# Single accumulation banks handed out by the ordering pass, per-head maxima, last 768 tokens by 384, new bookings

## The chip, the cores and the metric

The kernel runs on one core of a Trainium2 chip. The metric is the device time of one execution in microseconds (us). TensorE (PE in the profile) does the matrix products and the transposes, VectorE (DVE) and ScalarE (ACT) the elementwise work and all copies out of PSUM, SyncE (SP) issues the DMAs. GpSimd builds some constants at the start and does nothing else.

## The reference

Attention with a memory term, then two feed-forward layers, all float32:

```python
# per batch (4) and head (8): S = 576 tokens, D = 64
scores = q @ k.T / 8, causal mask, minus the row's maximum
a      = exp(scores); a /= a.sum(-1) + 1e-9
local  = a @ v
q_p    = where(q > 0, q, exp(q) - 1) + 1
mem    = (q_p @ M_prev) / (q_p . z_prev + 1e-6)
x      = sigmoid(beta) * mem + (1 - sigmoid(beta)) * local   # 2304 tokens x 512
h = x @ w_in;  x = (h * tanh(softplus(h))) @ w_out            # 512 -> 2048 -> 512
h = x @ w_in2; out = (h * cos(h)) @ w_out2                    # 512 -> 2048 -> 512
```

## The kernel before

Two heads make a pair; 16 pairs (four of each batch) are worked one after the other. For each pair q and k are loaded and transposed on TensorE (tiles ptq, ptk), scores of five row blocks are made in three slots (tile s, `f_sc`; the mask is added by small products, line 495), VectorE takes the row maxima (tile nm, `f_mx`), ScalarE the exponentials with their sums (tile p, `f_ex`), VectorE scales the rows (line 572) and writes the memory columns (line 549). The blocks of p are then transposed (tile t, `flip`, 30 transposes for a pair), copied out into PT by ScalarE or VectorE, and multiplied with v and M_prev (tile pv). The result xs goes to DRAM (x1d).

The first layer runs in two parts. `block0` ("phase 0") takes blocks of 256 tokens through the first 8 of the 16 slices of 128 hidden units: products into h (line 759), copy to g, the activation, a split of g into a high and a low half G, products into acc (line 802), and the partial sums to DRAM (xad). `late` with p = 1 ("phase 1") takes blocks of 384 tokens through the other 8 slices (lines 887 and 967) and adds the partial sum (line 978); with p = 2 ("phase 2") it does the second layer, all 16 slices (lines 887 and 969). Each float32 product is three passes of split operands. Weights are loaded and decoded by five operations each (`weight`, lines 125 to 142); those of slices 8 to 15 can only be placed once the attention's memory is given back (`f_host`).

No engine's order is written by hand. Every operation is a task with engine(s), a booked cost, dependences, a rank and the buffers that it takes; `arrange` lets a greedy pass run over a booked clock and emits, on each engine, the ready task of lowest rank. Attention ranks before phase 0, phase 0 before phases 1 and 2, so phase 0 fills what the pass books as idle on TensorE. Tasks marked "act/dve" go to whichever engine is free in the books. A class of buffers has a fixed number of places (`slots_of`); in PSUM the eight banks are split by class: sc 2 places of two banks, misc 2, h 1, acc 1. Until the first phase-0 product, `arrange` puts dummy products (line 303, tile warm) where the booked load of TensorE is low. Once emitted, each engine takes its instructions strictly in that order.

## Time and profile before

| | |
|---|---|
| three timed runs | 1083.94, 1082.56, 1082.08 us; median 1082.56 us |
| profiled execution, first to last instruction (span) | 1080.1 us; it comes with no other time of its own, and the timed runs lie 2.0 to 3.8 us above its span |
| TensorE busy | 1053.2 us (98%), 6938 products |
| VectorE busy | 761.6 us (71%) |
| ScalarE busy | 570.1 us (53%) |
| attention (last pv ends) | 373 us |
| phase 0 ends, phase 1 begins | 481 us |
| phase 2's first acc product | 686 us |

Engines work at the same time, so their busy times do not add up. Products are pipelined: a row's mean duration is the time from a product's start to its end, and the next one starts before that end; how fast products really follow each other is read from a run of them in the chain of waits (its length divided by its count). A wait names the instruction that waited and the one that released it.

### The profile page before, as it was taken

The numbers are of one execution on the slowest core, as the hardware profiler recorded it, in microseconds if no ns is written. First come the engines' busy times: TensorE is split into PE (matmuls) and PEld (weight loads), VectorE is DVE, ScalarE is ACT, GpSimd is POOL, SyncE is SP. The second block draws the span as 40 slices with busy tenths as digits, with TensorE's granted clock in tenths as the row PEclk, the third lists the DMA queues.
The fourth block names the chain that finished last, engine by engine and source line by source line (L and its number), as shares of the span: only waits on it lengthen the run. The fifth ranks groups of instructions, "written<-read, shape, count | busy, mean of one in ns | idle before, by whom it ended". The sixth has DMA issues, their size and how long they took to land.

```text
span 1080.1 us, 17930 instructions
## 1 busy us (share of the span) xinstructions
PE 1053.2 (98%) x6938; PEld 938.7 (87%) x6938; DVE 761.6 (71%) x1694; ACT 570.1 (53%) x1279; POOL 3.8 (0%) x19
## 2 busy tenths in 40 slices
PE   8898999999999999999999999999999999999998
PEld 5666778788877899989999999998999999999997
DVE  6999997886787568757552228887666676766664
ACT  4676675676676443433323234766555555555544
POOL 1000000000000000000000000000000000000000
PEclk9999999999999999999999999999999999999999
DMA  6455423222322165446352216211000010000000
GB/s 165 114 132 161 113 55 103 69 70 67 100 69 59 44 204 156 137 135 205 102 183 88 89 59 187 79 38 59 1 30 30 1 59 2 30 30 1 30 1 30
DMA packets 112853, 88.73 MB, mean 82 GB/s; under 512 B 65792, under 2 KB 103680, under 8 KB 112768
## 3 DMA queue, kind: packets, MB, share of 16 engines
q1 hardware_dynamic: 112768, 87.58, 27.1%
q8 instruction: 55, 0.90, 0.3%
q14 instruction: 30, 0.25, 0.1%
HBM read 68.69 MB, written 18.87 MB: 81 GB/s over the span
## 4 chain that ended last, share of the span: by engine, by line
PE 88%; DVE 7%; ACT 3%; issue 1%; POOL 0%; ACTq 0%; POOLq 0%; DVEq 0%
PE h L887 28%; PE acc L969 18%; PE acc L967 9%; PE h L759 9%; PE acc L802 9%; PE pv L654 5%; PE t L587 4%; PE s L491 3%; DVE nm L520 2%; DVE p L572 1%; PE warm L303 1%; ACT p L536 1%; PE ptq L400 1%; ACT PT L315 1%; PE ptk L400 1%
## 5 line engine op out<-in xcount | busy, mean ns | idle before, releaser
L887 PE MATMUL h<-x,w 128*128 128x384 f32 x1728 | 345.0, 337 | 1.6 <-ACT g L903 1.6
L887 PEld LDWEIGHTS h<-x,w 128*128 128x128 f32 x1728 | 307.4, 188 | 17.2 <-ACT g L903 1.8
L969 PE MATMUL acc<-w,G 128*128 128x512 f32 x864 | 228.4, 393 | 0.0
L969 PEld LDWEIGHTS acc<-w,G 128*128 128x128 f32 x864 | 160.0, 188 | 22.1
L954 DVE TENSOR_TENSOR G<-g,G 128x384 fp32r<-128x384 f32 x144 | 79.8, 555 | 100.2 <-ACT G L315 99.6
L759 PE MATMUL h<-x,w 128*128 128x256 f32 x864 | 127.7, 288 | 4.6 <-DVE g L317 4.2
L802 PE MATMUL acc<-G,w 128*128 128x256 f32 x864 | 129.7, 289 | 1.1 <-ACT o L315 0.7
L759 PEld LDWEIGHTS h<-x,w 128*128 128x128 f32 x864 | 111.4, 191 | 9.0 <-DVE g L317 5.2
L315 ACT ACTIVATE G<-g 128x384 fp32r<-128x384 f32 (+1 forms) x152 | 81.2, 535 | 66.6 <-DVE g L938 35.8
L802 PEld LDWEIGHTS acc<-G,w 128*128 128x128 f32 x864 | 111.9, 191 | 4.0 <-ACT o L315 1.4
L967 PE MATMUL acc<-G,w 128*128 128x384 f32 x576 | 112.6, 336 | 0.0
L536 ACT ACTIVATE p<-s,nm 128x64 f32<-128x64 f32 (+4 forms) x160 | 81.3, 515 | 40.0 <-DVE nm L520 26.2
L967 PEld LDWEIGHTS acc<-G,w 128*128 128x128 f32 x576 | 100.9, 188 | 0.0
L931 ACT ACTIVATE n<-n 128x384 f32<-128x384 f32 x96 | 49.9, 521 | 63.5 <-DVE n L927 63.5
L903 ACT ACTIVATE g<-h 128x384 f32<-128x384 f32 x48 | 23.4, 491 | 113.1 <-PE h L887 112.2
L587 PE MATMUL t<-ident,p 128*128 128x128 f32 (+1 forms) x480 | 73.7, 277 | 7.8 <-ACT PT L315 3.7
L520 DVE TENSOR_REDUCE nm<-s 128x2 f32<-128x1024 f32 (+4 forms) x80 | 62.2, 790 | 23.5 <-PE s L495 16.4
L915 DVE TENSOR_SCALAR u<-hs 128x384 f32<-128x384 f32 x96 | 34.5, 359 | 54.6 <-ACT hs L315 51.9
L938 DVE TENSOR_TENSOR g<-n,hs 128x384 f32<-128x384 f32 x96 | 53.2, 555 | 26.3 <-ACT n L934 26.2
L587 PEld LDWEIGHTS t<-ident,p 128*128 128x128 f32 (+1 forms) x480 | 52.3, 140 | 18.5 <-ACT PT L315 7.8
L315 ACT ACTIVATE hs<-h 128x384 f32<-128x384 f32 x96 | 47.0, 490 | 39.3 <-PE h L887 36.6
L315 ACT ACTIVATE PT<-t 128x256 f32<-128x256 f32 (+3 forms) x97 | 43.4, 466 | 42.0 <-PE t L587 41.5
(91 smaller groups left out, 1243.6 us busy)
## 6 DMA issues: line engine op xcount, KB each, us to landing
raw<-in_moe_w_in_dram SPq DMA_DIRECT2D x32, 512.0 KB, 4.3
raw<-in_moe_w_out_dram SPq DMA_DIRECT2D x32, 512.0 KB, 3.8
k<-in_k_dram SPq DMA_DIRECT2D x32, 144.0 KB, 2.8
x1d<-xs SPq DMA_DIRECT2D x32, 144.0 KB, 2.1
xad<-o SPq DMA_DIRECT2D x9, 512.0 KB, 3.7
x2d<-o SPq DMA_DIRECT2D x6, 768.0 KB, 3.6
x<-x2d SPq DMA_DIRECT2D x6, 768.0 KB, 4.2
out_dram<-o SPq DMA_DIRECT2D x18, 256.0 KB, 2.0
```

What stands on the lines that cost most here:

```text
L315: nc.scalar.activation(dst, src, AF.Copy, scale=1.0 if scale is None else scale)
L520: nc.vector.tensor_reduce(out=s["nm"][:, c], in_=s["sp"][i], axis=AX.X, op=ALU.max, negate=True)
L536: nc.scalar.activation(d["p", i][:, j, D + lo:D + hi], src, AF.Exp, bias=s["nm"][:, c, j:j + 1], scale=1.0, accum_out=s["sm"][:, 1 if part ...
L587: nc.tensor.transpose(ps[:, at:at + r], d["p", i][0:r, h, j * P:(j + 1) * P], ident[0:r, 0:r])
L654: nc.tensor.matmul(o[h * D:(h + 1) * D, z_ - lo:w], vt[:, h, j - 1, :] if j else d["mv"][:, h, :], PT[:, c + z_:c + hi], start=j == 0, sto ...
L759: nc.tensor.matmul(h[:, half // 2], w[:, a, 0, c * P:(c + 1) * P], x[:, e_, c, :], start=c == 0 and pi == 0, stop=c == NKC - 1 and pi == 2)
L802: nc.tensor.matmul(t[:, c], w[:, a, 1, n * P:(n + 1) * P], G[:, e_, half], start=f == 0 and pi == 0 and c == 0, stop=f == NFH - 1 and pi == 2,
L887: nc.tensor.matmul(q_["h"], w[:, a, 0, c * P:(c + 1) * P], x[:, e_, c, :], start=c == 0 and pi == 0, stop=c == NKC - 1 and pi == 2)
L938: nc.vector.tensor_tensor(out=q_["g"], in0=q_["n"], in1=q_["hs"], op=ALU.mult)
L954: ENG[e].tensor_tensor(out=q_["G"][:, 1], in0=q_["g"], in1=q_["G"][:, 0].bitcast(F32), op=ALU.subtract)
L967: nc.tensor.matmul(o, w[:, a, 1, c * P:(c + 1) * P], G[:, e_, :], start=st, stop=sp_)
L969: nc.tensor.matmul(o, G[:, a, c * P:(c + 1) * P], w[:, e_, 1, :], start=st, stop=sp_)
```

## The change

Five things are changed. (1) The fixed split of PSUM goes; `arrange` hands out eight single banks, with a cap for each class (`CAP`). (2) The scores of a pair's two heads stand in two banks taken one by one, the maximum is taken per head (two reductions of half the width in place of one), all maxima of a slot stand in the books ahead of the exponentials, and the exponentials of a head need only that head's maxima. (3) `block0` runs over 6 blocks of 256 tokens (1536 tokens) in place of 9; the last 768 tokens go through all 16 slices in blocks of 384, as the first two blocks of phase 1, without a partial sum. (4) Costs and latencies in the books are others, and instructions of VectorE and ScalarE may overlap by `NEXT`. (5) On TensorE a ready task of the same array mode (scores, pv, all others) now goes first whatever its rank (`KEEP`).

```diff
-    SEM, SWITCH, TABLE, WAIT = 0.1, 0.12, 1.3, 2.5
-    RATE, LAND = 160.0, 2.0
+    CAP = {"warm": 1, "sc": 4, "misc": 3, "h": 2, "acc": 4, "hB": 3}
+    def bank(b, name):
+        return pools["bank"][b.bank].tile([P, 512], F32, tag="b", name=name)
+    SEM, SWITCH, TABLE, WAIT = 0.035, 0.1, 1.28, 2.5
+    RATE, LAND, KEEP = 160.0, 2.0, 10000.0
+    TAIL = {"pe": 0.16, "act": 0.0, "dve": 0.0, "sp": 0.0, "host": -SEM}
+    NEXT = {"pe": 0.0, "act": -0.1, "dve": -0.09, "sp": 0.0, "host": 0.0}
...
+                    for x, o in enumerate(banks):
+                        y = clear(o) if x not in used else None
+                        if y is not None and (f is None or y < f):
+                            f, b.bank = y, x
+                    if n[b.cls] >= CAP[b.cls]:
+                        return None
...
+                    if e == "pe" and t.mode == mode:
+                        rank -= KEEP
...
-            bs, bp, bn = Buf("sc"), Buf("pt"), Buf("nm")
+            bs, bp, bn = [Buf("sc"), Buf("sc")], Buf("pt"), Buf("nm")
...
-                nc.vector.tensor_reduce(out=s["nm"][:, c], in_=s["sp"][i], axis=AX.X, op=ALU.max, negate=True)
+            for j in range(2):
+                for c, i in enumerate(SLOTS[x]):
+                        nc.vector.tensor_reduce(out=s["nm"][:, c, j:j + 1], in_=s["sp", i, j], axis=AX.X, op=ALU.max, negate=True)
+                maxed[j] = t_m
...
-    FS = (range(0, NFH), range(NFH, NF), range(0, NF))
-    blocks = [(p, j) for p in range(3) for j in range(NT // TBS[p])]
-    N0 = NT // T0
+    N0 = 6
+    NS = N0 * T0 // T1
+    JS = [*range(NS, N1), *range(NS)]
+    blocks = [(0, j) for j in range(N0)] + [(p, j) for p in (1, 2) for j in JS]
+    def FS(p, j):
+        return range(NA if p == 0 else NF) if p != 1 or j >= NS else range(NA, NF)
...
-                  "raw": 3, "dec": 2, "x": 2, "o2": 1, "hB": 3, "G2": 3, "g2": 2, "hs": 4, "u": 2, "n": 3,
-                     "acc1": 1, "acc2": 1, "acc3": 1, **{f"w{f}": 1 for f in range(NF)}})
```

How the instructions stand on the engines, before and after, at three places. First VectorE, from the first maximum of pair 12 on (nm12_0 and nm12_1 are the maxima of its first two slots). Before:

```order
L520 TENSOR_REDUCE nm12_0_3814<-s12_0_3789 128x2 x2
L317 COPY xs11_3800<-pv11_1_3803 128x288
L428 TENSOR_SCALAR mn13_3832<-q13_3775 128x640
L317 CAST G0_3_0_3837<-g0_3_0_3551 128x512
L317 CAST G0_3_1_3844<-g0_3_0_3551 128x512
L779 TENSOR_TENSOR G0_3_0_3837<-g0_3_0_3551,G0_3_0_3837 128x512
```

The same place after the change, where s12_0_0 and s12_0_1 are the banks of the two heads:

```order
L553 TENSOR_REDUCE nm12_0_3542<-s12_0_0_3510 128x1 x2
L553 TENSOR_REDUCE nm12_1_3548<-s12_1_0_3528 128x1
L553 TENSOR_REDUCE nm12_0_3542<-s12_0_1_3511 128x1
L355 COPY PT11_3501<-t11_4_3550 128x4x128
L355 COPY PT11_3501<-t11_4_3565 128x256
L553 TENSOR_REDUCE nm12_0_3542<-s12_0_1_3511 128x1
```

Each row block's maximum is two instructions, and the phase-0 work between (G0_3: block 3) is gone from here. Second TensorE, among the transposes of pair 11, before (acc0_2 and h0_3 belong to phase-0 blocks 2 and 3):

```order
L587 MATMUL t11_2_3730<-ident_85,p11_2_3635 128x128 x3
L802 MATMUL acc0_2_1_3607<-G0_2_3_3481,w0_6_1853 128x256 x6
L587 MATMUL t11_2_3746<-ident_85,p11_2_3635 128x128 x3
L587 MATMUL t11_1_3750<-ident_85,p11_2_3635 128x128 x2
L802 MATMUL acc0_2_1_3607<-G0_2_3_3481,w0_7_2005 128x256 x6
L587 MATMUL t11_1_3761<-ident_85,p11_2_3635 128x128 x2
L400 MATMUL ptq12_1_3765<-ident_85,q12_3463 128x128 x2
L759 MATMUL h0_3_1_3571<-x3_2724,w0_3_1262 128x256 x6
```

And after:

```order
L625 MATMUL t11_4_3565<-ident_85,p11_1_3394 128x128 x2
L803 MATMUL h0_2_0_3570<-x2_2778,w0_0_498 128x256 x6
L625 MATMUL t11_2_3580<-ident_85,p11_2_3470 128x128 x3
L625 MATMUL t11_2_3587<-ident_85,p11_2_3470 128x128 x3
L625 MATMUL t11_1_3592<-ident_85,p11_2_3470 128x128 x2
L803 MATMUL h0_2_0_3570<-x2_2778,w0_0_498 128x256 x6
L625 MATMUL t11_1_3605<-ident_85,p11_2_3470 128x128 x2
```

Here phase 0 is at its block 2 where it was at block 3 before. Third TensorE, at the end of phase 0, before (block 8 is its last):

```order
L759 MATMUL h0_8_3_5941<-x8_5466,w0_7_2005 128x256 x6
L802 MATMUL acc0_7_1_5864<-G0_7_3_5780,w0_7_2005 128x256 x6
L759 MATMUL h0_8_3_5941<-x8_5466,w0_7_2005 128x256 x6
L802 MATMUL acc0_8_0_5987<-G0_8_0_5890,w0_0_444 128x256 x6
L802 MATMUL acc0_8_0_5987<-G0_8_0_5890,w0_1_693 128x256 x6
L802 MATMUL acc0_8_0_5987<-G0_8_1_5898,w0_2_1037 128x256 x6
```

And after (block 5 is its last):

```order
L803 MATMUL h0_5_3_5313<-x5_4790,w0_7_1960 128x256 x6
L849 MATMUL acc0_5_0_5331<-G0_5_1_5311,w0_3_1281 128x256 x6
L849 MATMUL acc0_5_1_5385<-G0_5_0_5309,w0_0_498 128x256 x6
L849 MATMUL acc0_5_1_5385<-G0_5_0_5309,w0_1_963 128x256 x6
L849 MATMUL acc0_5_1_5385<-G0_5_1_5311,w0_2_1044 128x256 x6
L849 MATMUL acc0_5_0_5331<-G0_5_2_5402,w0_4_1434 128x256 x6
```

After the last h product both sides of acc now have work that needs only the first half of G. Counted over the whole order: ahead of the last pv of pair 15 stand 940 phase-0 products before and 521 after; the dummies are 218 and 157; TensorE changes its array mode 135 and 101 times; waits of a TensorE instruction for an earlier one of TensorE are 34 and 79. Up to pair 7's last scaling the three engines have the same work to 1 us. VectorE, up to pair 15's last scaling, has 80 more maxima, and fewer of these: 10 of line 779, 8 copies to g, 9 copies to xs, 6 casts to G, 4 of line 734 (x), 3 copies to o. ScalarE has 11 function-table loads there in place of 19.

## Rows read from the trace of the kernel before

**Rows 1.** The page: busy us of each engine, share of the span, instructions.
```profile
PE 1053.2 (98%) x6938; PEld 938.7 (87%) x6938; DVE 761.6 (71%) x1694; ACT 570.1 (53%) x1279; POOL 3.8 (0%) x19
```

**Rows 2.** Busy time of each engine by stretch, instructions, granted clock, DMA share, GB/s.
```profile
25.50:104.00 78.50, 70.38 (x592) 48.32 (x591) 74.17 (x195) 51.85 (x164) 0.00 (x0) 1.00 0.53 139
104.00:175.00 71.00, 67.15 (x574) 54.69 (x573) 67.23 (x163) 48.76 (x136) 0.00 (x0) 1.00 0.33 86
175.00:373.00 198.00, 195.18 (x1665) 161.25 (x1663) 149.47 (x385) 125.58 (x331) 0.00 (x0) 1.00 0.26 70
373.00:481.00 108.00, 104.52 (x825) 101.68 (x824) 69.65 (x122) 41.29 (x64) 0.00 (x0) 1.00 0.47 149
```

**Rows 3.** Waits of VectorE, 25 to 175 us, the longest: total, times, longest one.
```profile
DVE g L317 <- PE h L759: 1.5, 3, 0.6
```

**Rows 4.** Waits of TensorE's products, 175 to 373 us, the longest.
```profile
PE pv L654 <- DVE PT L317: 1.3, 1, 1.3
```

**Rows 5.** VectorE's instructions in time around 174 us: start, length.
```profile
173.10 0.69 DVE L317 COPY PT<-t 128x512 f32<-128x512 f32 x1
173.71 0.90 DVE L572 TENSOR_SCALAR p<-p,sm 128x320 f32<-128x320 f32 x3
...
174.86 0.31 DVE L572 TENSOR_SCALAR p<-p,sm 128x192 f32<-128x192 f32 x1
```

**Rows 6.** The chain that ended last, pieces from 370 to 546 us: start, length.
```profile
370.80 2.26 PE pv L654 x20
...
395.22 1.44 PE acc L802 x12
...
465.22 0.73 PE h L759 x6
...
465.97 0.61 ACT g L315
...
469.50 3.02 PE acc L802 x23
...
483.18 4.16 PE acc L967 x24
...
543.58 3.14 PE h L887 x18
```

**Rows 7.** VectorE by line and shape: count, busy time, mean ns of one, idle before.
```profile
L520 DVE TENSOR_REDUCE nm<-s 128x2 f32<-128x1024 f32 x16 | 19.4, 1210 | 0.9 <-PE s L495 0.9
L520 DVE TENSOR_REDUCE nm<-s 128x2 f32<-128x128 f32 x16 | 4.6, 287 | 6.0 <-ACT p L536 6.0
L779 DVE TENSOR_TENSOR G<-g,G 128x512 fp32r<-128x512 f32 x36 | 23.2, 686 | 0.5 <-ACT G L315 0.4
L317 DVE COPY g<-h 128x512 f32<-128x512 f32 x17 | 11.7, 689 | 18.6 <-PE h L759 18.5
L317 DVE COPY xs<-pv 128x288 f32<-128x288 f32 x15 | 6.8, 452 | 3.8 <-PE pv L654 3.6
L317 DVE CAST G<-g 128x512 fp32r<-128x512 f32 x22 | 8.8, 422 | 13.5 <-ACT g L771 13.5
```

**Rows 8.** TensorE's products of line 759 alone, by stretch (products, then weight loads).
```profile
175.00:373.00 198.00, 53.24 (x354) 45.41 (x354) 1.00 0.26 70
373.00:481.00 108.00, 53.48 (x366) 47.64 (x366) 1.00 0.47 149
```

**Rows 9.** The same for line 802.
```profile
175.00:373.00 198.00, 56.72 (x363) 46.63 (x361) 1.00 0.26 70
373.00:481.00 108.00, 59.84 (x420) 54.34 (x420) 1.00 0.47 149
```

**Rows 10.** TensorE by line, 175 to 373 us: the transposes of p.
```profile
L587 PE MATMUL t<-ident,p 128*128 128x128 f32 (+1 forms) x250 | 37.3, 274 | 0.0
```

**Rows 11.** TensorE by line, whole span: the dummies, and products of line 802.
```profile
L303 PE MATMUL warm<-zeros,ident_b 128*128 128x256 bf16 x218 | 31.1, 285 | 2.0 <-DVE zeros L300 2.0
L802 PE MATMUL acc<-G,w 128*128 128x256 f32 x864 | 129.7, 289 | 1.1 <-ACT o L315 0.7 <-DVE G L779 0.3
```

More of the change, by code (lines that the diff above doesn't have):

```diff
@@ L39, in tile_kernel @@
     NF = DFF // P
-    NFH = NF // 2
+    NA = 8
     NJ = B * NP
@@ L212, in at_free, with room @@
                     return None
-                at = max(at, u.end + SEM)
+                at = max(at, u.end + u.lag + SEM)
+            return at
+        def room(t):
+            at, used, n, more = 0.0, [], {}, {}
+            for b in t.takes:
+                k = more.get(b.cls, 0)
+                more[b.cls] = k + 1
+                if b.cls != "misc" and b.n != turn[b.cls] + k:
+                    return None
+                if b.cls not in CAP:
+                    f = clear(held[b.cls][(turn[b.cls] + k) % len(held[b.cls])])
+                else:
+                    if b.cls not in n:
+                        n[b.cls] = 0
+                        for o in banks:
+                            if o is not None and o.cls == b.cls:
+                                f = clear(o)
+                                n[b.cls] += f is None or f > now
+                    f = None
+                    for x, o in enumerate(banks):
[3 more added lines that the diff above has]
+                    if n[b.cls] >= CAP[b.cls]:
+                        return None
+                    n[b.cls] += 1
+                    used.append(b.bank)
+                if f is None:
+                    return None
+                at = max(at, f)
             return at
@@ L267, in arrange @@
                     cost, mode = cost + (SWITCH if t.mode != mode else 0.0), t.mode
-                t.on, t.end = e, now + cost
-                free[e] = t.end
+                t.on, t.end = e, now + cost + TAIL[e]
+                free[e] = now + cost + NEXT[e] + (t.over if e != "pe" else 0.0)
                 if e == "pe":
-                    done.append((now, t.end))
+                    done.append((now, free[e]))
                 if t.size:
@@ L285, in arrange @@
                         put(d)
-                later(t.end)
+                later(free[e])
                 if e == "host":
@@ L302, in f_dummy @@
     def f_dummy(e):
-        nc.tensor.matmul(warm["w"][:, 0], ident_b, warm["z"], start=True, stop=True)
-    t_warm = add("dve", 0.2, f_warm)
+        nc.tensor.matmul(warm["w"][:, 0:T0], ident_b, warm["z"], start=True, stop=True)
+    b_warm = Buf("warm")
+    t_warm = add("dve", 0.2, f_warm, takes=[b_warm])
     def run(order):
@@ L819, in f_o @@
                 d["o"] = O(bi, NKC, T0)
-            copy(e, d["o"][:, 2 * side:2 * side + 2, :], d["acc"])
+            copy(e, d["o"][:, 2 * side:2 * side + 2, :], d["acc", side])
         e0 = add("act/dve", c_both(512), lambda e: f_o(e, 0), [lasts[0]], RM + bi, [bo], [ba[0]])
@@ L827, in block0 @@
         return lasts[1]
-    seq = [(bi, p, j, f) for bi, (p, j) in enumerate(blocks) if p for f in FS[p]]
     RL = 30000.0
@@ L858, in late @@
             sp.append(add("dve", 0.95, f_lo, [a], R0 - 60, [], [bx]))
-        ba = [Buf(f"acc{c}") for c in range(na)]
+        ba = [Buf("acc") for c in range(na)]
         bo = Buf("o2")
-        if p == 1:
+        part_ = p == 1 and j < NS
+        if part_:
             def f_xa(e):
@@ L1016, in tile @@
         def tile(self, shape, dt, tag, name):
-            return self.pool.tile(shape, dt, tag=tag, name=name, bufs=slots_of.get(tag, 3))
+            return self.pool.tile(shape, dt, tag=tag, name=name, bufs=slots_of.get(tag.rstrip("01"), 3))
     pools["a2"] = Own(attn.enter_context(tc.tile_pool(name="a2", bufs=2, side="right")))
-    ring = ExitStack()
-    pools["acc"] = ctx.enter_context(tc.tile_pool(name="accA", bufs=1, space=bass.MemoryType.PSUM, side="left"))
-    pools["h"] = ctx.enter_context(tc.tile_pool(name="hA", bufs=1, space=bass.MemoryType.PSUM, side="left"))
-    pools["sc"] = ring.enter_context(tc.tile_pool(name="sc", bufs=2, space=bass.MemoryType.PSUM, side="right"))
-    pools["misc"] = ring.enter_context(tc.tile_pool(name="misc", bufs=2, space=bass.MemoryType.PSUM, side="right"))
+    pools["bank"] = [ctx.enter_context(tc.tile_pool(name=f"bank{i}", bufs=1, space=bass.MemoryType.PSUM)) for i in range(8)]
     def f_beta(e):
@@ L1059, in tile_kernel @@
         pair(m)
-    for i in range(2 * NFH):
-        weight(i, 200.0 + 30.0 * i)
+    for i in range(2 * NA):
+        weight(i, W0 + W1 * i)
     prev = None
```

191 lines of the change are left out of this document (99 added, 92 removed).

## The prediction

> **What bounds the kernel now.** I read the page first. TensorE is busy 98% of the span [rows 1], and the reader may stop there; but busy is not the same as useful, since dummies and products that wait for the next in line count as well. So I cut the span into stretches [rows 2]. From 25.5 to 175 us (pairs 1 to 7; pair 7's last scaling starts at 174.86 [rows 5]) VectorE is busy 94.5% and 94.7% of the time, and its longest waits there come to 1.5 us in 150 [rows 3]: VectorE sets the pace, and TensorE is filled up with dummies (218 of them, 31.1 us [rows 11]). From 175 to 373 us, where pair 15's last pv ends (370.80 + 2.26 [rows 6]), it is the other way round: TensorE is busy 195.18 of 198.00 and VectorE only 149.47 [rows 2]; TensorE's longest wait for others is 1.3 us [rows 4]. Here TensorE sets the pace, because phase 0 is pushed in between: 354 + 363 = 717 of its products lie in this stretch [rows 8, 9]. From 373 to 481 us phase 0 finishes alone, with 786 products [rows 8, 9]. After 481 TensorE runs without a gap worth naming, and the change leaves the amount of that work per block alone.
>
> **The change part by part.** I write the time as the end of attention plus what is left for TensorE after it, since each engine's order is fixed.
>
> *Left after attention.* Before, this is 1080.1 - 373 = 707.1 us, with 786 products of 256 columns. Twelve follow each other in 1.44 us, so one takes 0.120 [rows 6]. By the order after the change 521 of 1152 are done by then, so 631 are left: 155 fewer, 155 x 0.120 = 18.6 us less. Added are the 768 tokens by 384: 2 blocks x 8 slices x 24 = 384 products; 18 of them take 3.14 us on line 887 and 24 take 4.16 on line 967 [rows 6], 0.174 and 0.173, so 384 x 0.1735 = 66.6 us more. Sum 707.1 - 18.6 + 66.6 = 755.1.
>
> The swap by itself (three blocks of 256 for two of 384) takes away 576 x 0.120 = 69.1 and adds 66.6: 2.5 us gained. The Trainium skill, page "TensorE: Matmul & The Clock Gate", section "Back-to-back issue gap", has a product cost its columns at 2.4 GHz plus 2.5 ns, which speaks against this part: 109.2 and 162.5 ns make 62.9 against 62.4 us, 0.5 us gained, and the sum would end 2.0 us later by it. The rows here show 11 ns more than that at either width, so they disagree.
>
> *The end of phase 0.* Before, the last h product begins its run at 465.22 for 0.73 us, and the first acc product that needs its result starts at 469.50: 465.95 to 469.50 = 3.55 us in which TensorE stands still behind copy, activation and split [rows 6]. After, three runs of six acc products on the other side (3 x 0.72 = 2.2 us) and one on this side stand in that place, as the order shows. I take 3 us off (bounds 0 and 5.5, if other small waits of this stretch, which is busy 104.52 of 108.00 [rows 2], go as well). The wait at the change to phase 1 stays. 755.1 - 3 = 752.1.
>
> *Attention up to pair 7.* The order has the same work on all engines to 1 us (VectorE's more by that), and VectorE is already at 94.6%. I add 1 us: 176 in place of 175 (bounds 173, if exponentials that start earlier help, and 179).
>
> *Attention from pair 8 to the end.* This is the large term. TensorE's share falls: 521 - 276 = 245 phase-0 products stand here in place of 717 (276 stand ahead of pair 7's last pv). So what counts is VectorE's work. Before it is 149.47 [rows 2]. A row's length overlaps the next by 0.08 (0.69 long, next starts 0.61 later [rows 5]), so each instruction is priced at its mean less 0.08. The maxima: 1024 columns take 1210 ns and 128 take 287 [rows 7], so 1.03 ns a column and 155 ns fixed; splitting costs the fixed part, 0.075 with the overlap, x 80 = 6.0 us more. Fewer [rows 7]: 10 splits of line 779 at 0.606 = 6.1; 8 copies to g at 0.609 = 4.9; 9 copies of xs at 0.372 = 3.3; 4 splits of x and 3 copies to o, of the same 512 columns, at 0.61 = 4.3; 6 casts to G at 0.342 = 2.1. Together -20.7 + 6.0 = -14.7 (moves of under 1 us left out), all of it after pair 7: 134.8 us.
>
> How fast can VectorE get through 134.8? Its share in 104 to 175 us was 67.23 of 71.00 with TensorE at 67.15 of 71.00 [rows 2], so both can be near 95% at once; that gives 142.3. TensorE would now need: 198 - 717 x 0.120 = 112 us for 250/30 = 8.3 pairs before [rows 10], at most 13.4 a pair; 8 x 13.4 + 245 x 0.120 = 137. Two engines that both need 135 to 137 will wait on each other more, so I take 93%: 144.9 us (bounds: 139 at 97%, and 159 at 85%, halfway back to the 75% of the stretch as it was). Attention ends at 176 + 144.9 = 320.9.
>
> *What I cost at nothing.* The 45 additional waits of TensorE for itself: a bank's last user is many instructions back; if each had to see the product before it end, it would cost 289 - 120 = 169 ns [rows 6, 11], 7.6 us in all, and what hides them then is only the slack of a stretch that is bound by VectorE. The 34 mode changes and 8 table loads fewer: they are on engines that now wait (a saving of at most a few us where TensorE binds). The 61 dummies fewer: they stood in idle time.
>
> *Sum.* 320.9 + 752.1 = 1073.0 against a span of 1080.1: 7.1 us less. The median of the runs lies 2.5 above that span, so 1082.56 - 7.1 = **1075.5 us**.
>
> **The rivals.** *VectorE falls short.* With 472 phase-0 products gone from the stretch, nothing covers TensorE when VectorE is late, and ten maxima per pair in two chains give VectorE twice as many places to wait. It decides at a share of 134.8 / (1080.1 - 752.1 - 176) = 134.8 / 152 = 88.7%: below that the kernel is slower. At 87%, 154.9, it is 1085.5; at 85%, 158.6, 1089. For it: 75% is what VectorE had in this stretch. Against it: there it waited for a saturated TensorE, and where it did not, it reached 94.6%.
>
> *A trade.* Attention ends earlier by just as much as is left afterwards (share 88 to 90%): 1081 to 1084, no change to measure. The bank pool then did nothing but move phase-0 work behind attention. For it: the caps add up to more than eight banks, so during attention there is no more PSUM than before.
>
> *Better than that.* 97%, 3 us off the first stretch and the whole of the waits at the end of phase 0: 173 + 139 + 749.6 = 1061.6, that is 1064 as a median.
>
> *The clock falls.* The granted clock was 1.00 in every stretch [rows 2], with 218 dummies; now 157. If it went to 1.2 GHz in the early pairs, a pair's 13.4 us of TensorE would become 26.8, where pairs 1 to 7 took 149.5 / 7 = 21 us each: about 5 us a pair, an estimate from those two numbers; two such pairs bring 1085. No run of before shows the lower level. The same page of the Trainium skill, in its part on the clock gate, says that the slow clock is the default and activity lifts it, so fewer dummies point that way; the trace, always at full clock, neither confirms nor denies it.
>
> **How the numbers follow.** The forecast (attention ends between 317 and 326) has 0.52, the better case 0.18, the trade 0.13, VectorE short 0.12, the clock 0.05. A measurement of this kernel can tell about 0.2% (2.2 us) from no change. The first two are faster: 0.70. The trade is the same: 0.13. The others slower: 0.17. The range goes from 1065 (the better case but for its last us) to 1086 (VectorE at 87%); under 0.1 is left at either end. The forecast case by itself is 1071 to 1080.
>
> **What would show it.** In the profile after: pair 15's last pv ends near 321 us, against 373 (below 317: better; at 328 or beyond, no gain); VectorE's share from pair 8 to there is 92 to 95% and TensorE's below it; phase 0 ends near 403 us; TensorE stands still less than 1.5 us at its last acc products; products of 384 columns follow each other at 0.1735; the granted clock is 1.00 throughout; TensorE's waits for itself stay under 2 us. Wrong it would be made by a VectorE that waits for scores or for exponentials by more than 15 us between pairs 8 and 15, or by phase 0's last three blocks running with gaps, since 631 products at 0.120 assume none.

## The result and the profile after

The changed kernel takes 1062.61 us (median of 4 runs, 1062.04 to 1062.96), the kernel before in the same series 1082.32 (1081.57 to 1083.94). The ratio is 0.9819, 95% interval 0.9805 to 0.9833. The forecast was 1075.5 with a range from 1065, so the kernel is faster than the whole range: 19.7 us gained where 7.1 were forecast. The direction was right. One step was far off: attention up to pair 7, forecast 1 us longer, came out 6.5 us shorter; the other terms were off by 2.5 us or less.

The page, in answer to [rows 1]: busy us, share, instructions.

```profile
PE 1039.1 (98%) x6685; PEld 932.5 (88%) x6685; DVE 713.3 (67%) x1684; ACT 590.6 (56%) x1349; POOL 3.8 (0%) x19
```

The stretches, cut as in [rows 2]: near pair 0's last scaling and phase 0's first product (both cuts at the same times as there, since the events come at 27.1 and 105.9 us against 25.7 and 105.8), then at pair 7's last scaling, pair 15's last pv and phase 0's last product. Columns: length, then PE, PEld, DVE, ACT and POOL busy, granted clock, DMA share, GB/s.

```profile
25.50:104.00 78.50, 67.96 (x563) 49.13 (x561) 76.82 (x220) 53.17 (x170) 0.00 (x0) 0.98 0.57 150
104.00:168.50 64.50, 64.40 (x555) 53.37 (x552) 62.87 (x174) 48.12 (x130) 0.00 (x0) 1.00 0.34 91
168.50:310.75 142.25, 140.40 (x1237) 108.40 (x1233) 131.71 (x400) 104.64 (x309) 0.00 (x0) 1.00 0.33 82
310.75:393.40 82.65, 82.47 (x673) 82.11 (x668) 57.51 (x99) 30.25 (x47) 0.00 (x0) 1.00 0.54 166
393.40:1061.00 667.60, 663.35 (x3517) 624.50 (x3516) 367.75 (x740) 341.95 (x655) 0.00 (x0) 1.00 0.17 55
```

VectorE is busy 97.9%, 97.5% and 92.6% of the three stretches of attention, and TensorE 98.7% of the third at the same time. From 310.75 to 393.40, phase 0 alone, TensorE has 0.18 us of idle time where [rows 2] show 3.5. The events that cut the stretches, in the timeline: VectorE's last scalings of pairs 7 and 15, TensorE's last pv, and the last product of phase 0.

```profile
167.51 1.14 DVE L610 TENSOR_SCALAR p<-p,sm 128x320 f32<-128x320 f32 x4
...
302.59 0.54 DVE L610 TENSOR_SCALAR p<-p,sm 128x192 f32<-128x192 f32 x2
...
309.19 1.79 PE L692 MATMUL pv<-PT,v 128*64 128x288 f32 x16
...
392.27 1.24 PE L849 MATMUL acc<-G,w 128*128 128x256 f32 x9
```

So attention ends at 310.98, against 373.06 in [rows 6] and a forecast of 320.9; phase 0 ends at 393.5, against a forecast of 403. Products of phase 0 by stretch, for lines 803 and 849 alone (line 849 in the second row), in answer to [rows 8, 9]:

```profile
310.75:393.40 82.65, 38.23 (x288) 36.36 (x288) 1.00 0.54 166
310.75:393.40 82.65, 44.50 (x342) 42.58 (x342) 1.00 0.54 166
```

288 + 342 = 630 are left at the end of attention, as the order said (631). The longest waits of VectorE from pair 8 to pair 15's last scaling (168.5 to 303 us), then the longest of TensorE's products in 168 to 311 us (total, times, longest), in answer to [rows 3, 4]:

```profile
DVE nm L553 <- PE s L531: 2.1, 3, 1.0
DVE sm L595 <- ACT p L574: 0.8, 1, 0.8
...
PE t L625 <- DVE PT L355: 0.6, 3, 0.2
```

Both engines wait little, though each is needed nearly all the time: VectorE idles 6.4 us of those 134.5, TensorE 1.9 of the 142.25 up to the last pv. The chain of waits at the end of phase 0 and into phase 1, in answer to [rows 6]:

```profile
386.90 6.63 PE acc L849 x53
...
395.57 4.28 PE acc L1013 x23
400.88 2.09 PE acc L1013 x12
```

53 products in 6.63 us are 0.125 each, up to the end of phase 0; products of 384 columns follow at 2.09 / 12 = 0.174, as forecast (in the piece of 23 the first takes 0.279 to the next start, the others 0.173 to 0.185).

**Three sums for every kernel.** TensorE has work or dummies all the time, so I split the span by its products: R = end of attention less 0.120 for each product of phase 0 done by then; L = time from there to the end of phase 0, less 0.120 for each product left and 0.1735 for each of the 31 to 37 h products of phase 1 that stand there; E = the rest of the span. R holds attention's own products, the dummies and whatever is lost among them; L is what phase 0 loses when it runs alone. For the kernel before: R = 373.1 - 942 x 0.120 = 260.1; L = 479.2 - 373.1 - 786 x 0.120 - 36 x 0.1735 = 5.6; E = 1080.1 - 479.2 = 600.9. After: R = 311.0 - 522 x 0.120 = 248.4, L = 0.5, E = 667.6. The blocks by 384 move 576 x 0.120 = 69.1 us out of phase 0 and 66.7 into E, so E compares only between kernels of as many blocks. The fall of 19.0 us in the span is thus R 11.7, L 5.1 and the swap of blocks 2.3 (what is left without the two: 814.5 and 812.2), to 0.1 of rounding. The table has all runs; medians are of 4 to 6 runs, ratios against the kernel before, which ran at 1081.5 to 1082.6 us in the different series. R, L and E come from one profiled execution each, so their sum can differ from the median by 1 to 2 us.

| kernel | median us | ratio (95%) | attention ends | products left | R | L | E |
|---|---|---|---|---|---|---|---|
| before | 1082.3 | | 373.1 | 786 | 260.1 | 5.6 | 600.9 |
| after | 1062.6 | 0.9819 (0.9805, 0.9833) | 311.0 | 630 | 248.4 | 0.5 | 667.6 |
| after, old bookings | 1066.7 | 0.9856 (0.9843, 0.9869) | 335.6 | 462 | 252.8 | 0.1 | 667.0 |
| after, no mode preference | 1066.8 | 0.9855 (0.9842, 0.9868) | 320.5 | 576 | 251.4 | 0.4 | 667.7 |
| after, fixed PSUM | 1073.6 | 0.9925 (0.9908, 0.9943) | 335.2 | 450 | 250.9 | 4.9 | 669.5 |
| after, nine blocks | 1065.4 | 0.9842 (0.9829, 0.9855) | 311.6 | 1206 | 249.0 | 0.5 | 601.1 |
| after, maxima per row block | 1064.0 | 0.9842 (0.9828, 0.9856) | 316.5 | 594 | 249.5 | 0.1 | 667.6 |
| after, misc 2 banks | 1065.2 | 0.9844 (0.9831, 0.9858) | 344.4 | 372 | 250.8 | 0.6 | 667.6 |
| after, h 1 bank | 1077.5 | 0.9961 (0.9949, 0.9973) | 316.2 | 612 | 251.4 | 11.8 | 667.6 |
| after, more VectorE, pairs 0-3 | 1070.2 | 0.9890 (0.9876, 0.9904) | 317.3 | 618 | 253.3 | 0.0 | 671.5 |
| after, more VectorE, pairs 8-15 | 1066.4 | 0.9854 (0.9840, 0.9868) | 310.1 | 636 | 248.2 | 0.0 | 671.5 |
| after, small tile alone | 1066.9 | 0.9863 (0.9850, 0.9877) | 311.1 | 630 | 248.4 | 0.5 | 671.5 |
| after, 64-byte tile alone | 1065.9 | 0.9851 (0.9837, 0.9864) | 310.4 | 630 | 247.8 | 0.5 | 670.6 |
| before, new bookings | 1091.7 | 1.0091 (1.0078, 1.0105) | 348.0 | 1038 | 265.2 | 9.2 | 601.8 |
| before, maxima per head, ahead | 1096.1 | 1.0127 (1.0111, 1.0143) | 379.3 | 840 | 272.7 | 5.9 | 600.9 |
| before, maxima per head | 1090.8 | 1.0080 (1.0066, 1.0094) | 369.5 | 888 | 268.7 | 6.2 | 600.9 |
| pool and maxima per head | 1075.4 | 0.9933 (0.9920, 0.9945) | 349.3 | 978 | 259.3 | 0.2 | 600.1 |
| the same with new bookings | 1067.6 | 0.9861 (0.9846, 0.9876) | 307.5 | 1266 | 252.1 | 0.6 | 601.1 |
| after, weights later | 1057.0 | 0.9765 (0.9753, 0.9778) | 307.0 | 618 | 242.9 | 0.1 | 667.6 |
| after, weights later, h 3 banks | 1056.0 | 0.9754 (0.9741, 0.9768) | 305.0 | 630 | 242.3 | 0.2 | 667.6 |

The seventh column shows at once what the end of attention does not: where h of phase 0 has one bank, L is 4.9 to 11.8, and where it has two or three, 0.0 to 0.6.

### The profile page after: what moved, and what is told of

The parts are those of the page before. It is cut to its first block, busy times and chain, and to the rows that moved or that the text cites. A ratio compares the mean times of both kernels' runs of the same rounds, so it can differ in the third digit from the quotient of the medians.

```text
span 1061.1 us, 17494 instructions
## 1 busy us (share of the span) xinstructions
PE 1039.1 (98%) x6685; PEld 932.5 (88%) x6685; DVE 713.3 (67%) x1684; ACT 590.6 (56%) x1349; POOL 3.8 (0%) x19
## 4 chain that ended last, share of the span: by engine, by line
PE 80%; DVE 17%; ACT 1%; issue 1%; POOL 0%; POOLq 0%; DVEq 0%
PE h L934 31%; PE acc L1015 19%; PE acc L1013 13%; PE acc L849 6%; PE h L803 5%; DVE nm L553 4%; DVE p L610 3%; PE t L625 2%; PE pv L692 2%; DVE PT L355 2%; PE s L527 2%; DVE p L587 1%; DVE ph L471 1%; DVE mn L474 1%; DVE den L480 1%
## 5 line engine op out<-in xcount | busy, mean ns | idle before, releaser
L934 PE MATMUL h<-x,w 128*128 128x384 f32 x1920 | 385.9, 337 | 0.0
L1001 DVE TENSOR_TENSOR G<-g,G 128x384 fp32r<-128x384 f32 x160 | 88.6, 554 | 126.8 <-ACT G L353 126.5
L1013 PE MATMUL acc<-G,w 128*128 128x384 f32 x768 | 153.4, 336 | 0.5 <-DVE G L355 0.4
L574 ACT ACTIVATE p<-s,nm 128x448 f32<-128x448 f32 (+4 forms) x160 | 82.2, 520 | 41.8 <-DVE nm L553 27.7
L803 PE MATMUL h<-x,w 128*128 128x256 f32 x576 | 81.6, 288 | 0.0
L849 PE MATMUL acc<-G,w 128*128 128x256 f32 x576 | 80.9, 288 | 0.4 <-DVE G L826 0.4
L974 DVE SCALAR_TENSOR_TENSOR n<-u,hs 128x384 f32<-128x384 f32 x96 | 53.4, 557 | 39.6 <-ACT u L967 39.0
L553 DVE TENSOR_REDUCE nm<-s 128x1 f32<-128x448 f32 (+4 forms) x160 | 71.4, 464 | 2.2 <-PE s L531 2.1
L140 ACT ACTIVATE w<-dec 128x512 fp32r<-128x512 f32 x64 | 39.8, 628 | 44.6 <-DVE dec L131 43.5
L527 PE MATMUL s<-kT,qT 64*128 64x448 f32 (+4 forms) x320 | 60.0, 464 | 3.6 <-DVE qT L357 1.2
```

What stands on the lines that cost most here:

```text
L527: nc.tensor.matmul(o[j][:, at:at + main], qT[pr, s0:s0 + P], kT[pr, 0:main], start=True, stop=False)
L553: nc.vector.tensor_reduce(out=s["nm"][:, c, j:j + 1], in_=s["sp", i, j], axis=AX.X, op=ALU.max, negate=True)
L574: nc.scalar.activation(d["p", i][:, j, D + lo:D + hi], src, AF.Exp, bias=s["nm"][:, c, j:j + 1], scale=1.0, accum_out=s["sm"][:, 1 if part ...
L803: nc.tensor.matmul(h[:, half // 2], w[:, a, 0, c * P:(c + 1) * P], x[:, e_, c, :], start=c == 0 and pi == 0, stop=c == NKC - 1 and pi == 2)
L849: nc.tensor.matmul(t[:, c], w[:, a, 1, n * P:(n + 1) * P], G[:, e_, half], start=f == 0 and pi == 0 and c == 0, stop=f == NA - 1 and pi == ...
L934: nc.tensor.matmul(q_["h"], w[:, a, 0, c * P:(c + 1) * P], x[:, e_, c, :], start=c == 0 and pi == 0, stop=c == NKC - 1 and pi == 2)
```

## The experiments

The theories, as they were numbered: 1, the bookings let VectorE work without gaps, and each us of VectorE in attention counts (the form of the prediction); 2, the pool of banks does it; 3, the grouping of array modes; 4, the swap of blocks; 5, TensorE's total decides, and VectorE counts only while TensorE has nothing but dummies; 6, the maxima ahead; 7, the parts work only together.

### One part undone at a time

Old bookings:

```diff
-    SEM, SWITCH, TABLE, WAIT = 0.035, 0.1, 1.28, 2.5
+    SEM, SWITCH, TABLE, WAIT = 0.1, 0.12, 1.3, 2.5
-    TAIL = {"pe": 0.16, "act": 0.0, "dve": 0.0, "sp": 0.0, "host": -SEM}
-    NEXT = {"pe": 0.0, "act": -0.1, "dve": -0.09, "sp": 0.0, "host": 0.0}
+    TAIL = {"pe": 0.0, "act": 0.0, "dve": 0.0, "sp": 0.0, "host": 0.0}
+    NEXT = {"pe": 0.0, "act": 0.0, "dve": 0.0, "sp": 0.0, "host": 0.0}
...
```

> The changed kernel with only the old bookings (costs, latencies, no overlap of instructions in the books); banks, maxima, blocks and mode preference stay. Theory 1 (the bookings: with them VectorE idles less in the pairs): most of the gain goes, 1072 to 1078 us, and VectorE idles about 1 us a pair again in pairs 1 to 7, against 0.2 to 1.0. Theory 2 (the pool of banks and the earlier maxima do it, whatever the books say): 1063 to 1066. By the order 690 products of phase 0 stand ahead of pair 15's last pv, against 522.

It took 1066.7 us, between the two theories: the bookings are worth 4.1 of the 19.7 us here. Pair 7's last scaling ends at about 182 us in place of 168.6, and attention 25 us later, but 168 more products of phase 0 are then done, so R rises by 4.4 only. From pair 0's end to pair 7's VectorE idled 5.5 us against 3.3, but above all it had more to do (149.4 us against 138.3). Two of its groups from 25.5 us to there (count, then busy us and mean ns):

```profile
L355 DVE COPY PT<-t 128x512 f32<-128x512 f32 (+3 forms) x28 | 15.2, 554 | 1.1 <-PE t L625 0.8
...
L355 DVE COPY xs<-pv 128x288 f32<-128x288 f32 x7 | 3.2, 456 | 0.2
```

In the changed kernel these are, up to the same event:

```profile
L355 DVE COPY PT<-t 128x256 f32<-128x256 f32 (+2 forms) x22 | 11.4, 523 | 0.7 <-PE t L625 0.7
...
L355 DVE COPY xs<-pv 128x288 f32<-128x288 f32 x1 | 0.4, 449 | 0.0
```

With the old bookings the pass gives more of the copies that either engine can make to VectorE, 6.6 us in these two groups.

No mode preference, and fixed PSUM:

```diff
-    RATE, LAND, KEEP = 160.0, 2.0, 10000.0
+    RATE, LAND, KEEP = 160.0, 2.0, 0.0
```

> The changed kernel without the preference for the same array mode: 134 mode changes in place of 102. Theory 1 and theory 2 both price this low: 32 changes at 0.1 us are 3 us if TensorE bound all of them, so 1062 to 1066. Theory 3 (grouping of modes is the gain, since every change drains TensorE): 1068 or more, and the pitch of the attention's products rises by more than 5 us in sum.

It took 1066.8 us: 4.2 more, a little above the range of 1 and 2, and below theory 3's 1068. Summed from each product's start to the next start, attention's own products take 210.3 us against 204.0, and dummies 26.6 against 30.2. Spread over 32 mode changes, the 6.3 us are 0.2 each; the intervals that cross a mode change, less the usual interval of a product of the same shape, make about 4.8 of them, so not all is the changes' own.

```diff
-    CAP = {"warm": 1, "sc": 4, "misc": 3, "h": 2, "acc": 4, "hB": 3}
+    CAP = {"warm": 1, "sc": 4, "misc": 2, "h": 1, "acc0": 1, "acc": 4, "hB": 3}
-        ba = [Buf("acc"), Buf("acc")]
+        ba = [Buf("acc0"), Buf("acc0")]
```

> The changed kernel with PSUM split as before during attention and phase 0 (scores 4 banks, misc 2, h 1, acc of phase 0 1); all else stays. Theory 1: only the end of phase 0 loses its cover, 3 us, so 1064 to 1067. Theory 2: 1070 to 1076, with VectorE and TensorE waiting on each other for banks in the pairs, and TensorE at a stand for 3 us again at the last acc products. By the order 702 products of phase 0 stand ahead of pair 15's last pv, against 522.

It took 1073.6 us: 11 more, as theory 2 said and against theory 1. The runs spread widely (1071.1 to 1076.9), and the profiled one was among the shorter: its span is 8.9 us longer than the changed kernel's. L is back at 4.9, R is 2.5 higher, and phases 1 and 2 lose 1.9. (The split is made by caps that add up to eight; the scores still take their banks one by one.)

Nine blocks, and the maxima in their old place:

```diff
-    N0 = 6
+    N0 = 9
```

> The changed kernel with all 9 blocks of 256 in phase 0, so none of the last 768 tokens by 384 alone. The order up to pair 15's last pv is the same. The sum says 576 x 0.120 against 384 x 0.1735: 2.5 us slower, 1064 to 1066. Theory 4 (the swap carries much of the gain, since the products of phase 0 run slower than 0.120 when they wait for a copy, an activation and a split, and the partial sums must be written and read back): 1069 or more.

It took 1065.4 us (1064.8 to 1066.1): the swap is worth 2.8 us, as the sum said (2.5). Theory 4 falls. The prediction set a figure of 0.5 us against this term. The Trainium skill's page "TensorE: Matmul & The Clock Gate", section "Back-to-back issue gap", gives the formula behind that figure for a product by itself, and says that in a stream of weight loads and products both set the spacing. Here there is one weight load to a product (PEld x6685 for PE x6685 in the page of the changed kernel), so the formula was applied to products that it is not meant for, and this run does not test it.

```diff
-            for j in range(2):
-                for c, i in enumerate(SLOTS[x]):
+            for c, i in enumerate(SLOTS[x]):
+                for j in range(2):
...
-                maxed[j] = t_m
+                maxed[c] = t_m
```

> The changed kernel with the maxima still taken per head, but in the old order: both heads' maxima of a row block, then its exponentials may start; in the change all maxima of a slot stand ahead. Theory 1 and 5: the order of the maxima matters little by itself, 1061 to 1065. Theory 6 (the maxima ahead keep ScalarE and VectorE from waiting for each other, and carry the gain): 1067 or more, with VectorE waiting for exponentials (sm <- p) by 5 us more in pairs 8 to 15.

It took 1064.0 us (1063.6 to 1066.8): 1.4 more. Theory 6 falls.

### Which class of banks

```diff
-    CAP = {"warm": 1, "sc": 4, "misc": 3, "h": 2, "acc": 4, "hB": 3}
+    CAP = {"warm": 1, "sc": 4, "misc": 2, "h": 2, "acc": 4, "hB": 3}
```

> The changed kernel with the class misc (transposes, pv) at 2 banks in place of 3, the others as changed. If the fixed split lost its 11 us because the pairs had too few banks for transposes and pv: 1069 to 1074, and 780 products of phase 0 ahead of pair 15's last pv show it in the order. If it lost them because h and acc of phase 0 had one bank each: 1062 to 1066.

It took 1065.2 us: misc is not the class. Attention ends at 344.4 us, 33 later than in the changed kernel, and the time is 2.6 longer: 258 more products of phase 0 are done by then. So the end of attention by itself does not tell the time.

```diff
-    CAP = {"warm": 1, "sc": 4, "misc": 3, "h": 2, "acc": 4, "hB": 3}
+    CAP = {"warm": 1, "sc": 4, "misc": 3, "h": 1, "acc": 4, "hB": 3}
```

> The changed kernel with h of phase 0 at one bank in place of 2, the others as changed. If h is where the fixed split lost: 1068 to 1073, with TensorE waiting for copies to g in the end of phase 0. If not: 1062 to 1066.

It took 1077.5 us, beyond the 1068 to 1073 that were expected: 14.8 of the 19.7 us are gone with one bank. Attention ends only 5 us later, R is 3.0 higher; L is 11.8 in place of 0.5. TensorE's longest waits in 316 to 408 us (total, times, longest), and below them four pieces of 4 us from there (columns as in the stretches):

```profile
PE acc L849 <- DVE G L826: 2.9, 5, 0.7
PE acc L849 <- ACT G L353: 2.3, 3, 1.7
PE acc L849 <- DVE G L355: 1.7, 1, 1.7
```

```profile
384.00:388.00 4.00, 1.75 (x10) 1.35 (x9) 3.93 (x8) 1.48 (x2) 0.00 (x0) 0.82 0.62 204
388.00:392.00 4.00, 4.00 (x28) 4.00 (x28) 3.71 (x7) 0.60 (x1) 0.00 (x0) 0.75 0.39 126
...
396.00:400.00 4.00, 2.26 (x17) 1.85 (x15) 1.05 (x3) 2.28 (x3) 0.00 (x0) 1.00 0.00 1
400.00:404.00 4.00, 3.28 (x16) 3.28 (x17) 0.67 (x2) 0.00 (x0) 0.00 (x0) 0.57 0.00 0
```

Products of acc wait 6.9 us for a split that could not be made earlier, because h had nowhere to stand until its copy was done. Twice TensorE has little to do (1.75 and 2.26 of 4 us) and the granted clock falls behind it, in part of the time to 1.2 GHz: 4 x (0.18 + 0.25 + 0.43) = 3.4 us more at most, so waits and clock together are up to 10.3 us of the 11.3 by which L rose. The rule of the Trainium skill, page "Perfetto Trace Analysis", section "Matmuls", that independent groups of products should rotate through banks so that emptying one overlaps filling the next, agrees with this run: 11.3 us of L for one bank less. Why the fixed split, also with one bank for h, loses only 4.9 there is not settled; it leaves 162 products fewer to that stretch, which is part of it.

### What a microsecond of VectorE costs

Sixteen reductions that nobody reads were added, in pairs 0 to 3 or in pairs 8 to 15:

```diff
+    more = const.tile([P, 1], F32, name="more")
...
+            def f_more(e):
+                nc.vector.tensor_reduce(out=more, in_=d["qT"][:, 0:512], axis=AX.X, op=ALU.max)
+
+            for _ in range((2, 1, 1)[x] if m < 4 else 0):
+                add("dve", c_dve(512), f_more, [t_s], S_ + 1, [], [B_["qT"]])
```

> The changed kernel with 16 additional reductions on VectorE, four in each of pairs 0 to 3, of 512 columns each, whose result nobody reads: 16 x 0.60 = 9.6 us more for VectorE, before the first product of phase 0 can stand. Theory 5 (what decides is TensorE's total, and VectorE counts only while TensorE has nothing but dummies): 7 to 11 us more than the changed kernel, 1069 to 1074. Theory 1 in the form of the prediction (each us of VectorE in attention delays its end by 1.05 us): the same, 1071 to 1073. By the order 179 dummies, against 157.

> The changed kernel with the same 16 reductions put into pairs 8 to 15, two in each. Theory 1 in the form of the prediction (each us of VectorE there delays the end of attention, and what is left after it stays): 1071 to 1073, since the order leaves about as many products of phase 0 behind it (648 against 642). Theory 5 (TensorE's total decides, VectorE has slack to give): at most 3 us more, 1062 to 1066. This and the run with the early ones tell the two apart.

They took 1070.2 and 1066.4 us. But E was 671.5 in both, 3.9 above the changed kernel's, where the other kernels of six blocks are within 0.6 of it but for the fixed PSUM's 669.5; no wait explains it. So the tile was tried alone:

```diff
+    more = const.tile([P, 1], F32, name="more")
+    nc.vector.memset(more, 0.0)
```

> A control for the two runs with additional reductions: the changed kernel with only their small result tile (128x1) added ahead of the weights' tiles and set to zero once, no reduction. In both those runs the products after phase 0 followed each other more slowly without any wait (667.5 us for 3514 of them against 663.5). If the shifted place of the tiles is the cause, this run shows the same 4 us, 1066 to 1067.5, and the late reductions cost nothing. If the reductions are the cause, it is at 1062 to 1063.5.

It took 1066.9 us with E = 671.5: the added tile, not the reductions, makes the 3.9 us. Against this control the early reductions cost 3.3 us (4.4 in the profiled spans) and the late ones -0.5, each for 9.6 us of VectorE. The prediction's form of theory 1 (1.05 us of time for each) falls in both halves of attention; theory 5 holds for the late half and overstated the early one (it said 7 to 11). VectorE itself did fall behind by the early ones: pair 7's last scaling ends at 179.0 us against 169.0 in the control. But attention ends only 6.2 us later, with 12 products fewer left behind it. The late run shows where its 9.6 us went, in VectorE's groups of 168.5 to 303.5 us:

```profile
L560 DVE TENSOR_REDUCE more<-qT 128x1 f32<-128x512 f32 x16 | 10.8, 676 | 0.0
L356 DVE COPY PT<-t 128x512 f32<-128x512 f32 x11 | 7.4, 678 | 0.1
L356 DVE COPY PT<-t 128x384 f32<-128x384 f32 x8 | 4.3, 551 | 0.0
```

The changed kernel has 15 and 11 of these two copies there. The pass gave the difference, and other copies, to ScalarE (105.79 us busy in that stretch against 98.38), and VectorE had no more to do than before (128.91 against 128.18).

```diff
-    more = const.tile([P, 1], F32, name="more")
+    more = const.tile([P, 16], F32, name="more")
```

> A control for the control: the changed kernel with an unused tile of 64 bytes a partition ahead of the weights' tiles, in place of one that takes 32. The weights of the first layer, x and G begin again at an odd multiple of 32 bytes, as in the changed kernel. If the place modulo 64 made the 4 us: 1062 to 1063.5. If any shift does: 1066 to 1067.5.

It took 1065.9 us, with E = 670.6: nearly the same loss, so the place modulo 64 bytes is not the cause; either of the two small shifts did it.

### Parts added to the kernel before

The new bookings alone, with one place for h as before:

```diff
+    TAIL = {"pe": 0.16, "act": 0.0, "dve": 0.0, "sp": 0.0, "host": -SEM}
+    NEXT = {"pe": 0.0, "act": -0.1, "dve": -0.09, "sp": 0.0, "host": 0.0}
...
-                t.on, t.end = e, now + cost
-                free[e] = t.end
+                t.on, t.end = e, now + cost + TAIL[e]
+                free[e] = now + cost + NEXT[e] + (t.over if e != "pe" else 0.0)
...
```

> The kernel before with only the new bookings (costs, latencies, overlap); fixed split of PSUM, both heads' maxima in one, nine blocks. If bookings work by themselves: 1076 to 1079, the 4 us that they were worth in the changed kernel. If they only work with the pool of banks: 1081 or more.

It took 1091.7 us, 1.0091 of before: slower. The bookings leave 1038 products behind attention in place of 786, and L is 9.2 us there in place of 5.6; R is 5.1 higher too, in attention's own products. TensorE idles 3.8 us of the stretch behind attention, where the changed kernel has 0.18 in its own:

```profile
348.00:488.00 140.00, 136.20 (x1074) 132.07 (x1074) 72.56 (x123) 55.05 (x83) 0.00 (x0) 1.00 0.38 120
```

The maxima per head, first ahead of the exponentials, then only split:

```diff
-                    nc.vector.tensor_reduce(out=s["nm"][:, c], in_=s["sp"][i], axis=AX.X, op=ALU.max, negate=True)
+            for j in range(2):
+                for c, i in enumerate(SLOTS[x]):
...
+                        nc.vector.tensor_reduce(out=s["nm"][:, c, j:j + 1], in_=s["sp"][i][:, j], axis=AX.X, op=ALU.max, negate=True)
```

> The kernel before with the maxima taken per head and all of a slot ahead of its exponentials, nothing else: 80 more reductions, 6.0 us more of VectorE by the price in the prediction. If VectorE's work decides: 1085 to 1089. If TensorE's total decides (VectorE waits 43 us in pairs 8 to 15 of that kernel): 1080 to 1084.

The first took 1096.1 us, 1.0127 of before, beyond both answers. VectorE has only 2.9 us more to do between pairs 0 and 15; R rises by 12.6, 9.1 of it as products of phase 0 that follow each other more slowly within attention. VectorE's split of g waits longer for ScalarE (total, times, longest; 13.5 us in all before, [rows 7]); that this wait slows the products was not tried:

```profile
DVE G L317 <- ACT g L774: 22.3, 6, 9.6
```

> The kernel before with the maxima taken per head but in the old order, row block by row block. With the maxima also ahead of the exponentials it was 13.5 us slower than before. If the 80 additional instructions did that: 1092 or more here too. If the order did, with one bank for h: 1082 to 1087, the price of the instructions alone.

The second took 1090.8 us, 1.0080 of before and between its two answers: about 9 us for the split, and 4 to 5 more for the place ahead. In the changed kernel the same place ahead gained 1.4.

Then all but the pool and the split undone in the changed kernel, and the same with the new bookings:

> The changed kernel with all but the pool of banks undone: old bookings, no mode preference, maxima per row block, nine blocks (the maxima stay per head). The parts undone one by one cost 4.1, 4.2, 1.4 and 2.8 us; if they add up, 1062.6 + 12.5 = 1075. If the pool carries the gain by itself: 1068 to 1072. If it needs the others (theory 7: the parts work only together, since the new bookings alone made the old kernel slower): 1079 or more.

> The same with the new bookings left in: pool and bookings, without mode preference, maxima ahead and the last 768 tokens by 384. If the parts add up: 1062.6 + 8.4 = 1071, 4 us less than the pool alone. In the kernel before, the same bookings cost 9.6 us; theory 7 has them turn from a loss into a gain with the second bank for h, since they push products of phase 0 behind attention (1266 of them by the order), where two banks let them run without a wait.

They took 1075.4 us, as the sum of the parts undone said, and 1067.6, 3 below it. Read as a way from before to after: the split 1082.3 to 1090.8, the pool to 1075.4 (R -9.4, L -6.0), the bookings to 1067.6 (R -7.2), modes, maxima ahead and the swap to 1062.6. So the same bookings are 9 to 10 us of loss with the fixed split and 7.7 of gain with the pool; theory 7 holds for them, and the pool is the largest part on this way. That it is the second bank for h, and not another part of the pool, that turns the bookings' sign was not tried by itself. The bookings also bring pair 7's last scaling forward, by 15.0 us in the pool and by 4.9 in the kernel before. These lines show its end in the pool without them, in the pool with them, and in the kernel before with them alone (175.2 without, [rows 5]):

```profile
183.12 0.31 DVE L610 TENSOR_SCALAR p<-p,sm 128x192 f32<-128x192 f32 x1
...
167.91 0.54 DVE L610 TENSOR_SCALAR p<-p,sm 128x192 f32<-128x192 f32 x2
...
170.00 0.31 DVE L574 TENSOR_SCALAR p<-p,sm 128x192 f32<-128x192 f32 x1
```

### A faster version

R still holds 157 dummies, all ahead of phase 0's first product. In pairs 0 to 3 VectorE also decodes weights, which are needed only later:

```diff
-    W0, W1 = 200.0, 30.0
+    W0, W1 = 400.0, 15.0
```

> The changed kernel with the decoding of weights ranked later (first rank 400 in place of 200, step 15 in place of 30), so that VectorE does less of it in pairs 0 to 3 and more in pairs 4 to 7. Theory 5: the first product of phase 0 comes earlier, dummies fall from 157 to 107 and some 50 x 0.12 = 6 us of them become useful time: 1057 to 1061. Theory 1 (VectorE's total up to pair 15 decides, and it is the same): 1062 to 1064.

It took 1057.0 us (1056.5 to 1057.1), 5.6 less than the changed kernel and all of it in R, as theory 5 said. Phase 0's first product starts at 99.2 us in place of 105.9, and 107 dummies are left. Then three banks for h as well:

> The kernel with the weights decoded later (1057.0 us) and three banks for h of phase 0 in place of two. If the second bank already took every wait out (products of phase 0 alone ran without excess at two): 1056 to 1058. If a third still helps inside attention, where these products cost 0.02 us more each: 1053 to 1055.5.

It took 1056.0 us (1055.5 to 1056.5): one us less, at the edge of the first answer, and no more than the series differ by. The dummies of the changed kernel (line 340 alone, 25.5 to 104 us):

```profile
25.50:104.00 78.50, 13.24 (x93) 8.82 (x93) 0.98 0.57 150
```

And of the kernel with weights later and three banks:

```profile
25.50:104.00 78.50, 6.86 (x43) 3.96 (x43) 1.00 0.56 145
```

This kernel takes 2.5% less time than the kernel before (ratio 0.9754, 0.9741 to 0.9768).

## Why the prediction was wrong

**The step that failed is "Attention up to pair 7".** I wrote "the same work on all engines to 1 us ... and VectorE is already at 94.6%. I add 1 us: 176 in place of 175 (bounds 173 ... and 179)". Measured: 168.6, outside the bounds. Of the 11.9 us by which the span was missed (1073.0 forecast, 1061.1 measured), 7.4 lie here, 2.5 in the next step and 2.0 behind attention; one more us is the distance from span to median, 1.5 here in place of 2.5. From pair 0's last scaling to pair 7's (141.6 us against 149.5) VectorE had 3 us less to do (138.3 against 141.4, its rows summed without overlap) and idled 3.3 us in place of 8.1. I took 94.6% for a ceiling; it was what that order reached. The sum had no term for the new bookings and the mode preference, and the runs put the difference on them: pair 7's last scaling ends at 182 us with the old bookings and at 175 without the mode preference, but at 166 with the fixed PSUM and at 170 with the maxima in their old place; in the pool without the other parts the bookings take it from 183 to 168.

**"Attention from pair 8 to the end" was right in share and a little high.** 144.9 forecast, 311.0 - 168.6 = 142.4 measured; work 131.7 against 134.8, share 92.6% against 93%. TensorE's share was not below it, as I had written, but 98.7%, and 9.6 us more for VectorE cost nothing here. So the figure came out of the share of an engine that did not set the time; that it was near is luck in part. Together the two steps put the end of attention 9.9 us too late: R 258.4 (320.9 - 521 x 0.120) in place of 248.4. Summed from start to start, the 11.7 us by which R fell are dummies (33.1 to 30.2), attention's own products (206.1 to 204.0) and what products of phase 0 take above 0.120 within attention (16.4 us for 942, 9.8 for 522). The last is the largest, and the forecast counted it as TensorE's need of the pairs (13.4 us each).

**What the runs put in its place.** VectorE's work is not the price: 9.6 us more of it cost nothing late, where the pass moved copies to ScalarE, and 3.3 early, though pair 7 then ended 10.0 us later. And the end of attention is not the aim: three kernels that end it 24 to 33 us later than the changed one are 2.6, 4.1 and 11 us slower, one that ends it 5 us later is 14.8 slower. The rival "VectorE short", with its break-even share of 88.7%, asked the wrong engine.

**"The end of phase 0"** was mis-sized: 3 us off, bounds 0 and 5.5; L fell by 5.1. The place was right (one halt at the last acc products), but the second bank of h also took out small waits on the way. "631 products at 0.120" held: L is 0.5.

**"Left after attention"** held: 752.1 forecast, 1061.1 - 311.0 = 750.1. The swap was 2.5 by the sum, 2.4 in the spans and 2.8 in the run with nine blocks.

**"What I cost at nothing".** The additional waits of TensorE for itself: right, none shows among its products' waits, and 1.2 us in all among those of its weight loads. Mode changes: wrong by 4.2 us when undone. Table loads and dummies were not separated.

**The maxima**, 6.0 us of VectorE in my sum, cost the kernel before about 9 us of time by the split. In the changed kernel the heads' maxima were never put together again, so what they cost there is not known.

**The rivals.** "Better than that" (1064, chance 0.18) was nearest, for the wrong reason: for the first stretch it took 173 (168.6 measured), and from pair 8 on 97% (92.6% measured). "A trade" and "VectorE short" did not come. "The clock falls" came briefly: the granted clock is 0.98 in 25.5 to 104 us, and these two pieces of 4 us hold the fall:

```profile
92.00:96.00 4.00, 2.59 (x18) 1.91 (x19) 3.93 (x13) 3.98 (x15) 0.00 (x0) 0.84 0.70 183
96.00:100.00 4.00, 3.98 (x25) 3.60 (x26) 3.29 (x9) 2.12 (x7) 0.00 (x0) 0.74 1.07 254
```

That is at most 4 x (0.16 + 0.26) = 1.7 us at full speed, in a stretch where VectorE is busy 97.9% and TensorE 86.6%.

**What stays open.** Each kernel is one order out of a greedy pass, and any edit redraws it: differences of 1 to 4 us between two of them can't be given to the edit alone. The 11 and 14.8 us of the banks, the 9 to 10 of the bookings in the kernel before and the 9 of the split stand well above that. How much of the fall in R is the pool's and how much the bookings' was read from one way through the parts; the other ways were not run whole.

## What to carry to other kernels

Where one engine is busy all the time, cost a change in that engine's time, by kind: its useful products at their undisturbed pace, and what it loses in each stretch. The end of a stage is a bad aim when filler work can move across it. A single accumulation bank for a chain of product, copy, activation and split can make good changes of order look bad: all three that were tried on it here made it slower, and one of them, the bookings, gains with the pool. Give it the second bank first, then judge bookings and priorities.

## What the hardware showed that was not expected

A tile of 128x1 ahead of the weights' tiles, which moves the tiles behind it by a few bytes and changes no order and no wait, made the 3500 products after phase 0 slower by 3.9 us in sum (E 671.5 against 667.6), about 1.1 ns each on average; a tile of 64 bytes cost 3.0. The loss is not even. From start to start, 768 acc products of 384 columns rise from 174.2 to 176.4 ns (1.7 us in sum), 863 acc products of 512 from 231.5 to 232.9 (1.2 us), and 1883 h products only from 175.2 to 175.7 (1.0 us). Stretches after phase 0 in that first control (PE busy as before, only longer):

```profile
393.50:660.00 266.50, 265.94 (x1513) 265.36 (x1512) 109.19 (x191) 90.06 (x169) 0.00 (x0) 1.00 0.29 95
660.00:1065.00 405.00, 401.32 (x2006) 361.97 (x2004) 259.34 (x550) 252.69 (x486) 0.00 (x0) 1.00 0.08 29
```

Not all tiles move (those placed from the other end stay), so the place of the operands relative to each other may matter; which one does was not tried. A probe that adds a tile needs a control that adds the tile alone. The granted clock also fell within a stretch of real products (0.57 at 400 to 404 us with one bank for h) right after a piece of 4 us in which TensorE was busy 2.26 us. So such a wait can cost more than its length: in that run the clock took up to 3.4 us on top of 6.9 us of waits.
